# The last sums of regrouped rows on VectorE, and two regrouping transfers asked for by GpSimd, at the end of a global-filter and SoLU kernel

## The chip, the cores and the metric

The kernel runs on one core of one Trainium2 chip. Its time is the device time of one execution in microseconds, and a kernel is judged by the median of its runs. The kernel before the change was run three times: 1555.18, 1557.51 and 1562.97 us, so its median is 1557.51 us. One more execution was profiled; every row of the profile below is from that one.

Five engines work beside each other: PE (TensorE, the matmuls, with PEld for its weight loads), DVE (VectorE), ACT (ScalarE), POOL (GpSimd) and SP (SyncE, which here only issues DMA transfers). Each takes its instructions in the order in which the program puts them. DMA transfers are issued by SP, ACT or POOL, and all of them run on the same 16 DMA engines.

## The reference, cut to what matters

```
# x: 8 x 3136 x 256; filters: 1569 x 256; 25088 tokens of 256 afterwards
X = rfft(x, axis=1);  y = irfft(X * (filt_r + 1j * filt_i), n=3136, axis=1)
t = y.reshape(25088, 256)
h = t @ w_in                                  # 25088 x 1024
sm = exp(h - max(h)) / (sum(exp(h - max(h))) + 1e-9)
solu = h * sm
ln = (solu - mean(solu)) / sqrt(var(solu) + 1e-6) * g_ln
out = ln @ w_out                              # 25088 x 256
```

## The kernel before, in words

**Blocks, pairs, groups.** The tokens are cut into 196 blocks of 128. Two blocks are a pair (98 pairs, numbered 0 to 97) and four are a group. For a pair, both matrix products are done by Strassen's scheme in Winograd's form: seven products of half-size blocks in place of eight, at the price of sums of blocks ahead of them. `product` does the first matrix product (128x512 tiles), `project` the second.

**One step.** `step(k)` runs for k = 0 to 204 and writes down, engine by engine, everything of one step; the order of its lines is the order on every engine. A step does the first product of block k, exponential, normalization and square of blocks k-2 and k-3, and one half of the second product of an older pair. Spectrum work of later batches is spread over the steps. Block 195, the last, has its first product in step 195. Steps 196 to 204 have no new block: there the pairs 93 to 97 are brought to their end. They are called the tail here.

**From rows to the second product.** The 1024 values of a token lie along a row, and the second product needs them as columns. `turn(k)` (L945) transposes 32x32 pieces on DVE into the group's tile `turn`. When all four blocks of a group are turned, `regroup(p, i)` (L953) collects block i of pair p into a tile `solu_t`: four DMA transfers of 128 KB, one for each quarter of the destination's partitions. The pairs 96 and 97 belong to the same group, so all their 16 transfers become possible at the same moment, when block 195 is turned. In this document 96/0 and 96/1 are the two tiles of pair 96, and 96/1 q2 is the third quarter of the second.

**Sums and products of a pair.** `project_sums` (L991) makes four tiles of 128x512 out of the two: s1 = a21 + a22 and s2 = s1 - a11 in its step 0, a21 = a11 - a21 (called s3, in place) and s4 = a12 - s2 in its step 1. Here a11 and a12 are the halves of tile 0, a21 and a22 those of tile 1: s1 needs tile 1 alone, the other three need both. All go through `sum_of` (L853), which puts them on POOL. The second product of a pair is written 95:4 for product 4 of pair 95; each product is 8 matmuls of 128x128. An odd step has p:1 (a11), p:2 (a12), p:6 (s2) and p:7 (s3), the even step after it p:5 (s1), p:3 (s4) and p:4 (a22). Products 1, 6 and 5 add into one PSUM bank, 2, 7 and 4 into another, and product 3 of the last five pairs has one of its own.

**Between the products.** After some products the bank is read before the next product adds to it: `keep_out` (L1036, ACT) and `finish_out` (L1040, DVE) scale a bank by the rows' deviation and add. Thus p:4 waits for the `finish_out` that reads the second bank after p:7, and (p+1):2 waits for the `finish_out` that reads it after p:4. `regroup_deviations` (L984) uses PE for a small matmul between two pairs, whose result ACT copies; (p+1):1 comes after that copy. `store_out` (L1045) writes a pair's result to memory with two transfers by SP.

**The tail's order.** Step 198 has, among others, on POOL: s1 and s2 of pair 95, then s3 and s4 of pair 95, then the transfers 97/1 q2 and q3, then the three small operations of `deviations` (L975). On DVE: one `finish_out` of pair 94, `turn(195)`, and the two remaining `finish_out` of pair 94. On ACT: the transfers 96/1 q0 and q1. On SP: 96/0 q0 to q3, 96/1 q2 and q3, 97/0 q0 to q3, 97/1 q0 and q1, then the stores. Step 199 has 95:1, 95:2, 95:6 and 95:7. Step 200 begins with s1 and s2 of pair 96; then come 95:5, the `finish_out` ahead of 95:4, 95:3, 95:4, the small matmul, s3 and s4 of pair 96, and the last two `finish_out` of pair 95. Step 201 has 96:1, 96:2, 96:6 and 96:7, and step 202 does for the pairs 96 and 97 what step 200 did for 95 and 96. Steps 203 and 204 are the products of pair 97.

**Waits of transfers.** A transfer counts on a semaphore when it has landed. SP and ACT share eight such semaphores, taken in turn, so that an issue can also wait until the transfer that had the same semaphore before has landed.

Of the kernel before, what the change touches and what calls it, by code (L numbers as in the profile page):

```python
# [13 lines left out]
ALU = mybir.AluOpType  # L14
# [96 lines left out]
def kernel(  # L111
# [10 lines left out]
    nc = tc.nc  # L122
# [727 lines left out]
    def tokens(k, c):  # L850
        return y[:, c, P * (k % NT):P * (k % NT) + P]

    def sum_of(out, in0, in1, op):  # L853
        nc.gpsimd.tensor_tensor(out=out, in0=in0, in1=in1, op=op)  # L854

    def pair_sums(j):

# [95 lines left out]
    def regroup(p, i, dma=nc.sync.dma_start, parts=range(4)):  # L953


        g, second = divmod(p, 2)
        turned = turns[g].rearrange("p (k q) b i -> p k q (b i)", q=4)
        a = 2 * second + i
        if (p, i) not in regrouped:
            if p == last[-1]:  # L960
                st = pools["r"].tile([P, KF, P], FP32, name=f"solu_t_{p}_{i}", tag="r")
            else:
                st = upool.tile([P, KF, P], FP32, name=f"solu_t_{p}_{i}", tag=f"solu_t{i}")
            regrouped[p, i] = st
            solu_ts[p, i] = st[:, 0:KF // 2, :], st[:, KF // 2:KF, :]
        for q in parts:
            dma(out=regrouped[p, i][32 * q:32 * q + 32, :, :], in_=turned[32 * a:32 * a + 32, :, q, :])  # L967
# [23 lines left out]
    def project_sums(p, step):  # L991

        (a11, a12), (a21, a22) = solu_ts[p, 0], solu_ts[p, 1]
        if step == 0:
            s1 = upool.tile([P, KF // 2, P], FP32, name=f"u1_{p}", tag="u1")
            s2 = spool.tile([P, KF // 2, P], FP32, name=f"u2_{p}", tag="u2")
            sum_of(s1, a21, a22, ALU.add)
            sum_of(s2, s1, a11, ALU.subtract)
            solu_sums[p] = s1, s2
        else:  # L1000
            s4 = spool.tile([P, KF // 2, P], FP32, name=f"u4_{p}", tag="u4")
            s1, s2 = solu_sums[p]
            sum_of(a21, a11, a21, ALU.subtract)
            sum_of(s4, a12, s2, ALU.subtract)
            solu_sums[p] = s1, s2, a21, s4

    def project(p, m):
# [136 lines left out]
    pairs = blocks // 2  # L1144

    def step(k):
        j, odd = divmod(k, 2)
        p = j - (LAG - 1) // 2 if odd else j - (LAG + 1) // 2
        if not 0 <= p < pairs:
            p = None  # L1150
        hid, proj = k < blocks, p is not None
        sums_of_x = differences[k] + products[k]
        if not odd and k > LAG:
            for job in sums_of_x:
                job()
            sums_of_x = []
        if not odd and 2 <= j - 4 < pairs:
            project_sums(j - 4, 0)
        plain = j < DIRECT
        if plain:  # L1160
            direct(2 * j, odd)
            if k == 0:
                convert_w_out(0)
        elif k < LAG:
            if not odd:
                product(j, 1)
                keep(j, k, 0)
                product(j, 2)
                finish(j, k, 0, (k, 0), 1)
            else:  # L1170
                product(j, 5)
                keep(j, k - 1, 1)
                finish(j, k, 1, (k - 1, 1), 2)
        for job in top[k] + (sums_of_x + stores[k] if k < LAG else stores[k] + sums_of_x):
            job()
        if not odd and 0 <= j - 4 < 2:
            project_sums(j - 4, 0)
        if odd and DIRECT <= j + 1 < pairs:
            pair_sums(j + 1)
        if not odd:  # L1180
            if hid and k > LAG:
                product(j, 1)
                keep(j, k, 0)
            if 2 <= k < blocks:
                exponential(k - 2)
            if proj:
                project(p, 5)
                keep_out(p, 1, (1, 1) if p in last else (0, 1))
            if p in last:
                keep_out(p, 0, (0, 1))  # L1190
                finish_out(p, 1, 1, (1, 1), 1)
            if blocks <= k < blocks + 2:
                exponential(k - 2)
            if hid and k > LAG:
                product(j, 2)
            if 3 <= k < blocks + 3:
                turn(k - 3)
            if hid and k > LAG:
                finish(j, k, 0, (k, 0), 1)
            if proj and p not in last:  # L1200
                finish_out(p, 1, 1, (0, 1), 1)
            for job in early[k]:
                job()
            if k == 6:
                w_out_mean()
            if 3 <= k < blocks + 3:
                square(k - 3)
            if plain:
                direct(2 * j + 1, 0)
            elif hid:  # L1210
                product(j, 6)
                keep(j, k + 1, 0)
            if proj:
                project(p, 3)
                if p not in last:
                    keep_out(p, 0, (0, 1))
                project(p, 4)
            if j >= 4 and j % 2 == 0 and j - 4 < pairs:
                regroup_deviations((j - 4) // 2, places.pop(p) if proj else psum("ps_rs")[:, 0, 0:4])
            for job in spectrum_loads[k]:  # L1220
                job()
            if 0 <= j - 3 < pairs - 2:
                regroup(j - 3, 0)
                regroup(j - 3, 1)
            elif j - 3 == pairs - 2:
                regroup(j - 3, 1, nc.scalar.dma_start, range(2))
                regroup(j - 3, 0)
                regroup(j - 3, 1, parts=range(2, 4))
                regroup(j - 2, 0)
                regroup(j - 2, 1, parts=range(2))  # L1230
            if 0 <= j - 4 < pairs:
                project_sums(j - 4, 1)
            if j - 3 == pairs - 2:
                regroup(j - 2, 1, nc.gpsimd.dma_start, range(2, 4))
            if 0 <= j - 3 < pairs and j % 2:
                deviations((j - 3) // 2)
            if hid and not plain:
                product(j, 7)
            if p in last:
                finish_out(p, 0, 1, (0, 1), 2)  # L1240
                finish_out(p, 1, 0, (1, 0), 1)
                store_out(p)
            if 2 <= k < blocks + 2:
                normalize(k - 2)
            for job in second_parts[k] + middle[k] + first_parts[k]:
                job()
            if proj and p not in last:
                finish_out(p, 1, 0, (1, 0), 1)
                store_out(p)
        else:  # L1250
            if hid and k >= LAG:
                product(j, 5)
                keep(j, k - 1, 1)
                finish(j, k, 1, (k - 1, 1), 2)
            for job in early[k]:
                job()
            if proj:
                project(p, 1)
                keep_out(p, 0, (0, 0))
                project(p, 2)  # L1260
                finish_out(p, 0, 0, (0, 0), 1)
            if 2 <= k < blocks + 2:
                exponential(k - 2)
            if plain:
                direct(k, 1)
            elif hid:
                product(j, 3)
                product(j, 4)
            if proj:
                project(p, 6)  # L1270
                project(p, 7)
            for job in second_parts[k] + middle[k]:
                job()
            if 3 <= k < blocks + 3:
                turn(k - 3)
            if hid and not plain:
                finish(j, k - 1, 1, None, 0)
                finish(j, k, 0, (k, 0), 2)
            if 2 <= k < blocks + 2:
                normalize(k - 2)  # L1280
            if proj:
                keep_out(p, 1, (1, 0))
            if 3 <= k < blocks + 3:
                square(k - 3)
            for job in first_parts[k]:
                job()
        if k == 6:
            center_w_out()
        if 7 <= k < LAG:
            for n in range(2 * k - 14, 2 * k - 12):  # L1290
                weight_sum(nc.vector, w_out_sb, n)
        for job in late[k] + loads[k]:
            job()
        if k == 5:
            weight_sum(nc.vector, w_in_sb, 3)
            w_out_sums()
        if k < 3:
            convert_w_out(k + 1)
        for n in {1: (0,), 2: (1,), 3: (2,), 4: (3,)}.get(k, ()):
            scale_w_out(n)  # L1300
        if k == 4:
            nc.gpsimd.dma_start(out=turn_t, in_=turn_dram)
# [35 lines left out]
```

## Time and profile before

| | |
|---|---|
| three runs | 1555.18, 1557.51, 1562.97 us |
| profiled execution, its own time | 1558.44 us |
| its span, first to last instruction | 1556.7 us |
| mean granted TensorE clock | 0.997 |
| PE busy | 1534.5 us (99%) |
| DVE, POOL, ACT busy | 1241.3, 1107.3, 923.3 us |
| tail: block 195 turned on DVE | 1526.61 us |
| tail: last matmul ends | 1551.45 us |
| POOL tensor_tensor, 128x512, alone | 1.26 us |
| DVE tensor_tensor, 128x512, both inputs in SBUF (L172), alone | 0.68 us |

Times in the tables and rows count from the start of the span. A row of the timeline has its start, its length, the engine, the source line, the operation with out<-in by the program's tile names (`u` for the sums, `solu_t` for regrouped tiles, `turn` for turned blocks, `ot` and `o` for the results), the count of instructions merged in it, and in brackets the idle time of the engine before it with what ended that. SPq and ACTq are the engines' sequencers, which issue transfers. A row of the stretches has, behind the stretch, its length and the busy time of PE, PEld, DVE, ACT and POOL with the count of instructions, then the granted TensorE clock (1.00 is full speed), the mean busy share of the 16 DMA engines and the GB/s that they moved.

### The profile page before, as it was taken

Reading aid. Unit: us, or ns where it says so; the run is one execution under the profiler, and the core shown is the slowest. Engines: PE = TensorE matmul, PEld = TensorE weight load, DVE = VectorE, ACT = ScalarE, POOL = GpSimd, SP = SyncE. Lnnn points to the kernel's source line nnn. Section 1 sums busy time; section 2 is a strip of 40 time slices with the busy share of each in tenths; the row PEclk is TensorE's granted clock in tenths of the full one; section 3 lists DMA queues with packets and bytes.
Section 4 is the critical chain, followed back from the end, with each engine's and each line's share of the span. In section 5 each row is a group of like instructions: output and inputs, shape, how many; then the busy total and the mean of one; then the engine's idle time right before and its main releaser. Section 6 shows DMA issues by size and latency. Waiting matters only on the chain. (4 is left out here: it accounts for less than half of the span.)

```text
span 1556.7 us, 36704 instructions
## 1 busy us (share of the span) xinstructions
PE 1534.5 (99%) x12922; PEld 1066.0 (68%) x12922; DVE 1241.3 (80%) x2220; ACT 923.3 (59%) x1893; POOL 1107.3 (71%) x1290
## 2 busy tenths in 40 slices
PE   9999999999999999999999999999999999999997
PEld 6735676666666776667666776667676777777777
DVE  5888878988988798868897699877987777777772
ACT  4556565665556565665656555665656656666662
POOL 2226776797879776986689678996767766676665
PEclk9999999999999999999999999999999999999999
DMA  9779587867986788667886678766874544344444
GB/s 250 267 254 274 160 229 218 238 196 212 245 242 188 188 247 238 198 164 202 248 230 183 166 209 246 209 181 185 228 206 118 135 122 121 97 119 105 107 109 109
DMA packets 340831, 297.58 MB, mean 191 GB/s; under 512 B 27313, under 2 KB 310731, under 8 KB 340649
## 3 DMA queue, kind: packets, MB, share of 16 engines
q1 hardware_dynamic: 277864, 175.33, 42.4%
q0 software_dynamic: 29152, 87.33, 18.7%
q10 hardware_dynamic: 33634, 32.58, 7.1%
q8 instruction: 105, 1.72, 0.5%
q14 instruction: 76, 0.62, 0.1%
HBM read 117.53 MB, written 74.84 MB: 124 GB/s over the span
## 5 line engine op out<-in xcount | busy, mean ns | idle before, releaser
L1022 PEld LDWEIGHTS o<-w_out_sb,solu_t 128*128 128x128 f32 x3136 | 381.7, 192 | 49.9 <-issue 43.1
L1022 PE MATMUL o<-w_out_sb,solu_t 128*128 128x128 f32 x3136 | 401.3, 276 | 3.7 <-DVE ot L1042 3.1
L1022 PEld LDWEIGHTS o<-w_out_sb,u 128*128 128x128 f32 x2352 | 307.3, 192 | 138.3 <-issue 108.6
L875 PE MATMUL m<-w_in_sb,s 128*128 128x512 f32 x760 | 384.5, 607 | 2.4 <-ACT h L896 1.6
L1022 PE MATMUL o<-w_out_sb,u 128*128 128x128 f32 x2352 | 310.7, 276 | 2.3 <-POOL u L854 1.8
L932 DVE SCALAR_TENSOR_TENSOR h<-e,h 128x1024 f32<-128x1024 f32 x196 | 304.5, 1554 | 0.0
L875 PE MATMUL m<-w_in_sb,y 128*128 128x512 f32 x570 | 297.1, 603 | 1.7 <-DVE h L907 1.2
L1038 ACT ACTIVATE ot<-o,rs_t 128x128 f32<-128x128 f32 x392 | 143.2, 367 | 244.6 <-PE o L1022 242.8
L896 ACT COPY h<-m 128x512 f32<-128x512 f32 x285 | 167.7, 588 | 200.5 <-PE m L875 179.7
L854 POOL TENSOR_TENSOR u<-solu_t 128x512 f32<-128x512 f32 x98 | 135.2, 1380 | 186.7 <-DMA solu_t<-turn 131.0
L910 DVE CUSTOM_DVE_ANT_0 h<-m,h 128x512 f32<-128x512 f32 x190 | 130.1, 685 | 166.8 <-ACT h L896 104.0
L940 ACT ACTIVATE h<-h,nmu 128x1024 f32<-128x1024 f32 x196 | 224.9, 1147 | 41.8 <-DVE turn L950 41.7
L950 DVE STREAM_TRANSPOSE turn<-h 128x1024 f32<-128x1024 f32 x196 | 243.2, 1241 | 3.2
L920 ACT ACTIVATE e<-h,nmax 128x1024 f32<-128x1024 f32 x196 | 225.3, 1149 | 9.3 <-DVE h L932 7.9
L854 POOL TENSOR_TENSOR u<-solu_t,u 128x512 f32<-128x512 f32 x98 | 136.9, 1396 | 99.6 <-PE o L1022 99.3
L1042 DVE SCALAR_TENSOR_TENSOR ot<-o,rs_t,ot 128x128 f32<-128x128 f32 x299 | 103.8, 347 | 100.1 <-ACT ot L1038 61.4
L875 PEld LDWEIGHTS m<-w_in_sb,s 128*128 128x128 f32 x760 | 124.5, 191 | 80.3 <-issue 63.0
L854 POOL TENSOR_TENSOR u<-u,solu_t 128x512 f32<-128x512 f32 x98 | 162.6, 1659 | 16.8 <-PE o L1022 7.6
L854 POOL TENSOR_TENSOR solu_t<-solu_t,solu_t 128x512 f32<-128x512 f32 x98 | 155.6, 1587 | 0.9
L875 PEld LDWEIGHTS m<-w_in_sb,y 128*128 128x128 f32 x570 | 93.6, 190 | 89.6 <-issue 45.9
L854 POOL TENSOR_TENSOR s<-y 128x128 f32<-128x128 f32 x190 | 94.4, 497 | 0.5
L437 PEld LDWEIGHTS py<-wb_t,t 50*64 50x64 f32 x3584 | 57.6, 134 | 42.9 <-issue 19.4
(153 smaller groups left out, 1939.0 us busy)
## 6 DMA issues: line engine op xcount, KB each, us to landing
solu_t<-turn SPq DMA_DIRECT2D x780, 128.0 KB
out_dram<-ot SPq DMA_DIRECT2D x196, 128.0 KB
t<-d POOLq DMA_DIRECT2D x112, 200.0 KB, 6.7
t<-d ACTq DMA_DIRECT2D x37, 512.0 KB
f<-f_dram POOLq DMA_DIRECT2D x37, 512.0 KB, 7.9
d<-g POOLq DMA_DIRECT2D x36, 512.0 KB, 4.8
d<-x POOLq DMA_DIRECT2D x80, 200.0 KB, 5.2
de<-de_tbl ACTq DMA_DIRECT2D x37, 256.0 KB
```

The costliest lines, as they stand in the source:

```text
L437: nc.tensor.matmul(out=views[g][64 * h:64 * h + 64, cb, i, :], lhsT=t4[rows, i, c0:c0 + 64], rhs=wb_t[rows, 0:N1], start=True, stop=True)
L854: nc.gpsimd.tensor_tensor(out=out, in0=in0, in1=in1, op=op)
L875: nc.tensor.matmul(out=ms[j, bank], lhsT=lhsT, rhs=w_in_sb[:, w, :], start=m in (1, 2, 7), stop=True, skip_group_check=True)
L896: nc.scalar.copy(out=h_half(k, i), in_=ms[j, 0])
L910: nc.vector.tensor_tensor_reduce(out=h_half(k, i), in0=ms[j, bank], in1=h_half(*kept), scale=1.0, scalar=sofar, op0=ALU.add, op1=ALU.min, ...
L920: nc.scalar.activation(out=e, in_=hs[k], func=AFT.Exp, bias=nmaxs.pop(k)[:, 1:2], scale=-1.0, accum_out=esums[g][:, i:i + 1])
L932: nc.vector.scalar_tensor_tensor(out=solu, in0=e, scalar=SHRINK, in1=solu, op0=ALU.mult, op1=ALU.mult, accum_out=nmu)
L940: nc.scalar.activation(out=solu, in_=solu, func=AFT.Square, bias=nmu, scale=-float(DFF), accum_out=variances[g][:, i:i + 1])
L950: nc.vector.transpose(out=turns[g][:, :, i, :], in_=solus[k].rearrange("p (f j) -> p f j", j=32))
L1022: nc.tensor.matmul(out=pos[p, bank], lhsT=lhs[:, f, :], rhs=w[:, f, :], start=f == 0 and (m in (1, 2, 7) or alone), stop=True, skip_group_ ...
L1038: nc.scalar.activation(out=out_half(p, *to)[0], in_=pos[p, 0], func=AFT.Copy, scale=rs)
L1042: nc.vector.scalar_tensor_tensor(out=ot, in0=pos[p, bank], scalar=rs, in1=out_half(p, *kept)[0], op0=ALU.mult, op1=ALU.add)
```

## The change

Three things change, all in the tail.

- `project_sums` gets an engine: VectorE where p + step is 96 or more. These are all four sums of the pairs 96 and 97, and s3 and s4 of pair 95. Each stays at the same place of the program's order, now in DVE's queue.
- The transfers 96/1 q2 and q3 are issued by POOL in place of SP. They stand in step 198 right behind the two that ACT issues, and so in POOL's queue behind s1 and s2 of pair 95.
- On SP, 97/0 follows directly on 96/0.

```diff
-    def sum_of(out, in0, in1, op):
-        nc.gpsimd.tensor_tensor(out=out, in0=in0, in1=in1, op=op)
+    def sum_of(out, in0, in1, op, engine=nc.gpsimd):
+        engine.tensor_tensor(out=out, in0=in0, in1=in1, op=op)
...
         (a11, a12), (a21, a22) = solu_ts[p, 0], solu_ts[p, 1]
+        engine = nc.vector if p + step >= pairs - 2 else nc.gpsimd
         if step == 0:
...
-            sum_of(s1, a21, a22, ALU.add)
-            sum_of(s2, s1, a11, ALU.subtract)
+            sum_of(s1, a21, a22, ALU.add, engine)
+            sum_of(s2, s1, a11, ALU.subtract, engine)
...
-            sum_of(a21, a11, a21, ALU.subtract)
-            sum_of(s4, a12, s2, ALU.subtract)
+            sum_of(a21, a11, a21, ALU.subtract, engine)
+            sum_of(s4, a12, s2, ALU.subtract, engine)
...
                 regroup(j - 3, 1, nc.scalar.dma_start, range(2))
+                regroup(j - 3, 1, nc.gpsimd.dma_start, range(2, 4))
                 regroup(j - 3, 0)
-                regroup(j - 3, 1, parts=range(2, 4))
                 regroup(j - 2, 0)
```

## The prediction

> **What bounds the kernel now.** First the page, for the engine that is always busy: it is PE, so only time in which PE idles or runs slowly can change.
>
> ```profile
> span 1556.7 us, 36704 instructions
> ...
> PE 1534.5 (99%) x12922; PEld 1066.0 (68%) x12922; DVE 1241.3 (80%) x2220; ACT 923.3 (59%) x1893; POOL 1107.3 (71%) x1290
> ```
>
> The change touches nothing ahead of step 198. Second, then, the chain that ended last, from 1520 us on: block 195 is turned at 1526.61, an ACT transfer and then an SP transfer land (1535.37), POOL makes s1, s2 and s3 of pair 96, and from 1539.41 on PE runs without a wait.
>
> ```profile
> 1527.70 3.52 DMA solu_t<-turn
> ...
> 1531.24 4.13 DMA solu_t<-turn
> ...
> 1536.87 1.26 POOL u L854
> 1538.13 1.23 POOL solu_t L854
> ...
> 1539.41 12.05 PE o L1022 x88
> ```
>
> Third, the timeline of the tail, for what each engine waits for: PE idles 0.56 us ahead of 95:6 (1529.01), 0.35 ahead of 96:1 (1534.40), 1.76 ahead of 96:6 (1538.18, for s2 of pair 96).
>
> ```profile
> 1525.51 2.94 PE L1022 MATMUL o<-w_out_sb,solu_t 128*128 128x128 f32 x24 [0.18 <-DVE ot L1042]
> 1526.53 0.57 DVE L1042 SCALAR_TENSOR_TENSOR ot<-o,rs_t,ot 128x128 f32<-128x128 f32 x2
> ...
> 1529.33 1.30 POOL L967 DMA_DIRECT2D solu_t<-turn  x2
> ...
> 1532.37 0.35 DVE L1042 SCALAR_TENSOR_TENSOR ot<-o,rs_t,ot 128x128 f32<-128x128 f32 x1 [3.12 <-ACT ot L1038]
> ...
> 1532.77 1.16 PE L1022 MATMUL o<-w_out_sb,solu_t 128*128 128x128 f32 x8
> ...
> 1534.40 2.02 PE L1022 MATMUL o<-w_out_sb,solu_t 128*128 128x128 f32 x16 [0.35 <-DMA solu_t<-turn]
> 1535.53 1.26 POOL L854 TENSOR_TENSOR u<-solu_t 128x512 f32<-128x512 f32 x1 [3.07 <-DMA solu_t<-turn]
> ...
> 1538.18 1.16 PE L1022 MATMUL o<-w_out_sb,u 128*128 128x128 f32 x8 [1.76 <-POOL u L854]
> ```
>
> Fourth, stretches of 3.41 us, for the clock: right after the stretch with that idle time, PE's granted clock is 0.50 for 3.41 us. The grid of stretches is set by the two times at which the clock changed. Three busy for 1.46 to 1.59 us of 3.41 (two of them shown) were followed by half clock; one busy for 1.86 was not. So a stretch in which PE idles for more than about 1.7 us costs half of the next 3.41 us, 1.7 us.
>
> ```profile
> 1536.27:1539.68 3.41, 1.59 (x12) 1.24 (x11) 0.35 (x1) 0.30 (x1) 3.33 (x4) 1.00 0.50 131
> 1539.68:1543.09 3.41, 3.41 (x18) 3.41 (x18) 0.00 (x0) 0.14 (x2) 3.33 (x3) 0.50 0.27 91
> ...
> 89.03:92.44 3.41, 1.46 (x4) 0.74 (x5) 3.38 (x7) 0.01 (x1) 0.00 (x0) 1.00 0.53 205
> 92.44:95.85 3.41, 3.41 (x6) 1.26 (x5) 3.17 (x8) 0.73 (x2) 0.00 (x0) 0.50 0.77 244
> 430.36:433.77 3.41, 1.86 (x5) 0.93 (x6) 2.66 (x6) 1.98 (x4) 2.04 (x3) 1.00 1.03 343
> 433.77:437.18 3.41, 3.41 (x41) 2.59 (x39) 3.38 (x6) 1.53 (x4) 1.38 (x3) 1.00 1.05 245
> ```
>
> **The change part by part.** *The length of a sum.* Ten sums of 1.26 us leave POOL. The same shape with both inputs in SBUF took DVE 0.68 us alone (L172); beside POOL's work the L172 rows reach a median of 1.16 and a maximum of 1.76. From 1531 us on POOL has nothing left to do, so I take 0.68, and 0.6 from start to start (DVE's rows overlap by 0.08).
>
> *s3 and s4 of pair 95.* They stand in DVE's queue between turn(195) and the last two finish_out of pair 94, the second of which frees the bank for 95:2. DVE is free at 1526.61, but POOL's s2 of pair 95 runs to 1526.94, and where a normalization on DVE started beside a sum on POOL (1503.06, 2.27 us against 1.22 alone) it ended one operation's length after POOL did. So s3 ends at 1527.6, s4 at 1528.2, the finish_out at 1528.5 and 1528.8 (before: 1527.1). 95:1 ends at 1527.35; 95:2 starts at 1528.8, an idle time of 1.45 us, and with it goes the 0.56 ahead of 95:6. PE is then 0.7 us behind, and 95:3 ends at 1533.3 (before: 1532.6). Bounds: 0 if DVE gets in beside POOL's last 0.3 us, 2.0 if POOL's transfer issues also hold it. None reaches the end, by the next step.
>
> *s1 and s2 of pair 96.* They now stand in DVE's queue ahead of the finish_out that 95:4 waits for (before: 1532.37, and 95:4 right behind it). s2 needs all of 96/0. Call the landing of its last transfer L; before, PE's 96:1 was released by it at 1534.3. s1 needs only 96/1 and runs earlier. So s2 ends at L + 0.7, the finish_out at L + 1.05, and there 95:4 starts: PE idles from 1533.3. From 95:4 to 96:1 it was 1.63 us (1532.77 to 1534.40: the small matmul and ACT's copy lie between), and that stays. Behind 96:1 come 14 products; at full clock one follows another by 0.895 us (1546.60 to 1548.39 for two), and the last takes 1.16, so the last matmul ends 1.63 + 13 x 0.895 + 1.16 = 14.4 us after 95:4's start, at L + 15.5. The waits of before inside this stretch go: s2, s3 and s4 of pair 96 are made beside 95:4 and 96:1. finish_out of pair 95, behind s3 and s4, ends at about L + 2.9, and 96:2 wants its bank at L + 3.6; pair 97's has less, some 0.1 us.
>
> *The transfers.* 96/1 q2 and q3 go out on POOL at 1527.0 instead of on SP at 1530.53 and 1531.24, and 97/1 q2 and q3 follow at 1528.3 and 1529.0 (0.65 each, from the 1.30 for two), instead of 1529.33 and 1530.03. By POOL's 3.8 to 4.2 us to landing 96/1 is complete at about 1532, not 1535.37. SP has ten issues instead of twelve, its stores of pair 94 come some 1.3 us sooner, and nobody waits for them. deviations on POOL moves up by 1 us, without effect.
>
> What it does to L is not in the trace. The 16 transfers moved 2.1 MB at 211 GB/s from 1528 to 1538 us, DMA share 0.73 to 1.13: the engines are the limit, and the change only reorders. Before, what had landed by L = 1534.3 were eight transfers, with two nearly done. Now 96/0 shares with the two of ACT and all four of POOL: ten. And SP's fourth issue waits for ACT's first transfer to land:
>
> ```profile
> SPq L967 <- DMA solu_t<-turn: 1.1, 1, 1.1
> ```
>
> Ten transfers of 131 KB at 211 GB/s from 1528.0 are 6.2 us, L = 1534.2; a wait for a slower landing of ACT's transfer pushes it. Lower end: the fourth issue at 1529.85 as before and 2.4 us to landing, as the first took on free engines, L = 1532.3. Upper end: ACT's first lands 2 us later (1531.9) and the fourth takes its 4.4 us of before, L = 1536.3. I take 1534.7, nearest to the row of before, with a little for four transfers on POOL ahead of it.
>
> *Clock.* With L = 1534.7 PE idles from 1533.3 to 1535.75 and again for 0.6 us ahead of 96:1. A grid of 3.41 us that lies anywhere has a stretch with over 1.7 us of that idle time in six cases of seven. So half clock once again, as in the profiled execution.
>
> *The sum*, against that execution: the last matmul ends at 1534.7 + 15.5 + 1.7 = 1551.9, where it ended at 1551.45. Behind it come the same finish_out, store and ends. 1558.44 + 0.45 = 1558.9 us. The profiled execution stands 0.9 us above the median of the runs, 1557.51; since it had the half clock and other runs may not have had it, I make no correction, and the forecast is 1.4 us above the median: no change that can be measured.
>
> **The rivals.** *The clock stays full.* The Trainium skill (TensorE: Matmul & The Clock Gate, the table on why this matters for your kernels) asks for idle gaps of over about 3 us before the clock falls; 1.8 us in 3.41 sufficed here, so the trace goes against it. As a mechanism of this kernel: the gap of 2.45 us is split by the grid, or too short, and nothing is lost. Then 1558.9 - 1.7 = 1557.2 us. For it: one case of seven by the grid, more if L is early; against it: the rows above.
>
> *The gain that DVE's shorter sums offer.* 96/0 lands by about 1532.3 to 1533, so DVE is through s2 before 95:3 ends, 95:4 waits little, and no stretch idles for 1.7 us. The last matmul ends at 1547.8 to 1548.5, 3.0 to 3.6 us sooner: 1554.8 to 1555.5 us. If DVE could run the finish_out ahead of s2, PE would be bound by the landing alone (96:1 at 1534.4, end 1547.2): 1554.2. For it: four transfers are asked for earlier, and SP's queue is shorter. Against it: the DMA engines are already full.
>
> *Slower: the wait on DVE is longer than the one on POOL that it replaces.* It decides from L = 1534.3 on with half clock, from 1535.9 without. POOL's transfers push those of SP: from 1531 to 1532 us, POOL's queue moved 0.12 MB with 32 packets and SP's 0.08 MB with 171. With L = 1536.3 it is 1560.5 us; if 96/0 came last of all 16, L = 1538.3, 1562.5. Against it: POOL's are 0.5 MB and pass in 2.5 us. The Trainium skill (DMA: Bandwidth & Descriptors, queues, rings and completion order) says that an engine takes whole packets from the queues in turn; those packets of some 4 KB against 512 B agree, and by that rule alone SP would have about a tenth of the engines until 1531.5, L about 1535.5 and 1559.7 us.
>
> **How the numbers follow.** Chances: the forecast 0.45 (L from 1533.8 to 1535.6 at half clock: 1558.0 to 1559.8), full clock 0.2, the gain 0.15, slower 0.2. The range takes in the middle of the gain and most of the slower case, and runs differ by some us among themselves (three span 7.8): 1553.8 to 1562.2. Less than 0.5% (7.8 us), about what a measurement of this kernel can tell from no change, is all that any case gives; the three idle times above and the slow clock together are 4.4 us. I leave 0.03 for faster and 0.04 for slower by more, for a spread of the runs like the one shown.
>
> **What would show it.** In the profile after: DVE rows of 0.68 us for the sums; PE idle ahead of 95:2 for about 1.4 us on a finish_out; PE idle ahead of 95:4 for about 2.4 us, ended by a finish_out that ran right behind s2; no idle time ahead of 96:6; 96/1 landed before 96/0; half clock for 3.41 us somewhere from 1536 on. It is wrong if 96/0 lands more than 1 us from 1534.7, if DVE's order differs from the program's, or if PE idles inside 96 and 97.

## The result, and the profile after

| | before | after |
|---|---|---|
| median of 22 runs each | 1559.62 us | 1563.45 us |
| ratio, 95% interval | | 1.0023 [1.0012, 1.0034] |
| profiled execution, its own time | 1558.44 us | 1565.15 us |
| its span | 1556.7 us | 1563.4 us |

The change made the kernel slower by 0.23%: 3.6 us by the ratio, 3.83 by the medians. That is under the 0.5% within which the prediction put any change, but it is a loss clear of the noise where no measurable change was forecast, and 1563.45 us lies above the range.

Block 195 was turned at 1526.60 us before and at 1529.40 us after. Those 2.8 us lie ahead of everything that the change touches; kernels that are alike up to there had it anywhere between 1525.28 and 1533.73 us in the executions profiled below. So all times of the tail below count from the end of that turn. "The tail" is from there to the end of the last matmul: 24.84 us before, 28.36 us after, 3.52 us more. So the two profiled executions show the size of loss that the medians show.

The page of after, its first lines: PE is still the engine that is always busy, DVE has the ten sums more; POOL has ten sums less and two transfer issues more.

```profile
span 1563.4 us, 36701 instructions
...
PE 1537.0 (98%) x12922; PEld 1069.0 (68%) x12922; DVE 1241.0 (79%) x2230; ACT 923.9 (59%) x1893; POOL 1097.2 (70%) x1282
```

The timeline of after's tail, with what each engine waited for:

```profile
1530.06 2.45 POOL L967 DMA_DIRECT2D solu_t<-turn  x4 [0.32 <-issue]
1530.21 0.68 DVE L854 TENSOR_TENSOR u<-solu_t,u 128x512 f32<-128x512 f32 x1
...
1531.46 1.16 PE L1023 MATMUL o<-w_out_sb,solu_t 128*128 128x128 f32 x8 [1.11 <-DVE ot L1043]
...
1535.54 0.69 DVE L854 TENSOR_TENSOR u<-solu_t 128x512 f32<-128x512 f32 x1 [2.47 <-DMA solu_t<-turn]
1539.83 0.69 DVE L854 TENSOR_TENSOR u<-u,solu_t 128x512 f32<-128x512 f32 x1 [3.60 <-DMA solu_t<-turn]
1540.44 0.35 DVE L1043 SCALAR_TENSOR_TENSOR ot<-o,rs_t,ot 128x128 f32<-128x128 f32 x1
...
1540.84 2.07 PE L1023 MATMUL o<-w_out_sb,solu_t 128*128 128x128 f32 x8 [4.64 <-DVE ot L1043]
```

PE waits twice: 1.11 us ahead of 95:2 (1531.46) and 4.64 us ahead of 95:4 (1540.84). Both waits name a `finish_out`. The second one stood on DVE behind s2 of pair 96 (1539.83), and s2 stood waiting 3.60 us for a transfer. The three waits of before (0.56, 0.35 and 1.76) are gone, ahead of 96:6 too. The chain that ended last says which transfer:

```profile
1532.79 6.92 DMA solu_t<-turn
...
1539.83 0.69 DVE u L854
1540.52 0.27 DVE ot L1043
...
1540.84 2.07 PE o L1023 x8
...
1543.13 14.64 PE o L1023 x112
```

It is 96/0 q3, SP's fourth, issued at 3.38 and landed 6.92 us later, at 10.31. Before, it was issued at 3.25 and landed at 7.66. Last the clock, in stretches on its own grid of 3.41 us (length, PE's busy time and matmuls, granted clock, DMA share, GB/s):

```profile
1532.68:1536.09 3.41, 3.41 (x32) 1.00 0.89 207
1536.09:1539.51 3.42, 0.10 (x1) 1.00 1.08 235
1539.51:1542.92 3.41, 2.08 (x10) 0.50 0.49 126
1542.92:1546.33 3.41, 3.41 (x16) 0.50 0.26 84
1546.33:1549.75 3.42, 3.42 (x32) 1.00 0.05 17
```

The long wait brought not one stretch at half clock, as before, but two.

### The profile page after: what moved, and what is told of

Its sections match the earlier page's. It is cut to its first block, busy times and chain, and to the rows that moved or that the text cites. A ratio compares the mean times of both kernels' runs of the same rounds, so it can differ in the third digit from the quotient of the medians.

```text
span 1563.4 us, 36701 instructions
## 1 busy us (share of the span) xinstructions
PE 1537.0 (98%) x12922; PEld 1069.0 (68%) x12922; DVE 1241.0 (79%) x2230; ACT 923.9 (59%) x1893; POOL 1097.2 (70%) x1282
## 5 line engine op out<-in xcount | busy, mean ns | idle before, releaser
L854 POOL TENSOR_TENSOR solu_t<-solu_t,solu_t 128x512 f32<-128x512 f32 x95 | 149.6, 1575 | 0.9
```

Of the source, the lines that this page charges most:

```text
L854: engine.tensor_tensor(out=out, in0=in0, in1=in1, op=op)
```

## The experiments

Two theories stood against each other. **A:** the loss is the place of s1 and s2 on DVE: the `finish_out` that frees 95:4's bank waits behind sums that wait for transfers, and POOL's transfers make the last one of 96/0 late. **B:** it is DVE's own work, or the transfers alone. (The expectations on record letter their theories anew for each run.) For each run: when 96/0 and 96/1 were complete, PE's idle time (waits over 0.08 us, summed), half clock inside the tail, the tail, the rest of it (PE's own time), and the kernel's median against that of the kernel before on the same chip.

| run | 96/0 | 96/1 | idle | half clock | tail | PE's own | median | ratio |
|---|---|---|---|---|---|---|---|---|
| before | 7.66 | 8.76 | 2.67 | 3.41 | 24.84 | 22.17 | | |
| before_again | 7.94 | 8.72 | 2.64 | 0 | 23.30 | 20.66 | -0.85 | 0.9991 [0.9976, 1.0005] |
| after | 10.31 | 6.12 | 5.75 | 6.83 | 28.36 | 22.61 | +3.83 | 1.0023 [1.0012, 1.0034] |
| after_again | 9.10 | 6.11 | 4.55 | 6.83 | 27.37 | 22.82 | +3.10 | 1.0017 [1.0002, 1.0032] |
| e1_sums_only | 6.74 | 8.22 | 4.44 | 6.83 | 27.41 | 22.97 | +3.17 | 1.0019 [0.9998, 1.0040] |
| e6_behind_sp | 6.63 | 8.16 | 1.55 | 0 | 22.56 | 21.01 | -1.81 | 0.9988 [0.9975, 1.0001] |
| e2_transfers_only | 7.55 | 6.72 | 0.84 | 0 | 21.75 | 20.91 | -3.39 | 0.9984 [0.9970, 0.9997] |
| e2b_transfers_only | 8.66 | 6.59 | 1.53 | 0 | 21.98 | 20.45 | -0.60 | 0.9991 [0.9975, 1.0006] |
| e3_sums_behind | 8.81 | 6.09 | 2.29 | 0 | 22.93 | 20.64 | +2.11 | 1.0017 [1.0000, 1.0035] |
| e3b_sums_behind | 8.87 | 6.11 | 2.36 | 3.41 | 24.63 | 22.27 | +2.01 | 1.0010 [0.9995, 1.0025] |
| e4_two_on_pool | 7.49 | 6.02 | 2.93 | 3.41 | 24.56 | 21.63 | +0.88 | 1.0000 [0.9984, 1.0016] |
| e7_fetch_early2 | 8.72 | 6.62 | 4.17 | 3.41 | 25.78 | 21.61 | +1.56 | 0.9997 [0.9982, 1.0012] |
| e8_fill | 8.74 | 6.59 | 1.11 | 0 | 24.50 | 23.39 | +0.56 | 1.0006 [0.9992, 1.0021] |
| e5_fetch_early | 9.33 | 6.67 | 4.77 | 6.83 | 27.49 | 22.72 | +13.87 | 1.0100 [1.0074, 1.0126] |

The last column but two sorts itself: 20.5 to 21.0 us without half clock in the tail, 21.6 to 22.3 with one stretch, 22.6 to 23.0 with two (e8 has 24 matmuls more). So a stretch of half clock costs 0.6 to 1.8 us, and two cost 1.6 to 2.5.

### One part of the change alone

**e1_sums_only**: the sums on DVE, the transfers by the same engines and in the same order as before. With s3 and s4 of pair 95 gone from POOL, its transfers 97/1 q2 and q3 still go out sooner, at 0.30 and 1.00 us where it was 2.73 and 3.43.

```diff
                 regroup(j - 3, 1, nc.scalar.dma_start, range(2))
-                regroup(j - 3, 1, nc.gpsimd.dma_start, range(2, 4))
                 regroup(j - 3, 0)
+                regroup(j - 3, 1, parts=range(2, 4))
```

> Only the sums go to VectorE; all transfers are issued as before the change. Lengths are counted from the end of the turn of block 195: the last matmul ended at 24.84 us before the change and at 28.36 after it; the last transfer of 96/0 landed (L) at 7.66 before and 10.30 after. Theory A (the order on VectorE makes PE wait for L, and the transfers on GpSimd make L late): L is as before, about 7.7; PE waits ahead of 95:4 until L + 1.1; the last matmul ends at L + 15.5 at full clock, 23.2, or 24.9 to 26.6 with one or two stretches of half clock. Theory B (the order on VectorE alone is the loss): about 28.4 whatever the transfers do. Theory C (the transfers alone are the loss): PE does not wait ahead of 95:4, 21 to 23 us.

**e2_transfers_only**: the two transfers of 96/1 by GpSimd, all sums on POOL, as before. The diff is against the kernel before.

```diff
                 regroup(j - 3, 1, nc.scalar.dma_start, range(2))
+                regroup(j - 3, 1, nc.gpsimd.dma_start, range(2, 4))
                 regroup(j - 3, 0)
-                regroup(j - 3, 1, parts=range(2, 4))
```

> Only 96/1 q2 and q3 go to GpSimd; all sums stay there, so that s3 and s4 of pair 95 run behind these two transfers and 97/1 q2, q3 behind the sums. Counted from the end of the turn of block 195. Theory A: no finish_out waits behind a sum, so 95:4 is not held; 96/1 lands at about 4 to 6 us, 97/1 is asked for 2.5 us later than in the changed kernel and passes behind 96/0, so L is 7.7 to 9; 96:1 starts at L and the last matmul ends at L + 12.9, 20.6 to 22 at full clock against 24.84 before: a gain of 2 to 4 us. Theory C (the transfers alone are the loss): L is about 10.3 as in the changed kernel, PE idles ahead of 96:1 by 2.6 us and the clock falls, 25 us or more.

**e1**: tail 27.41 us, above the 23.2 to 26.6 that theory A gave: I had left out that s1, at the head of DVE's queue, needs 96/1, which SP now brings last. The timeline:

```profile
1536.26 0.69 DVE L854 TENSOR_TENSOR u<-solu_t 128x512 f32<-128x512 f32 x1 [4.68 <-DMA solu_t<-turn]
1537.04 0.69 DVE L854 TENSOR_TENSOR u<-u,solu_t 128x512 f32<-128x512 f32 x1
...
1538.05 2.08 PE L1023 MATMUL o<-w_out_sb,solu_t 128*128 128x128 f32 x8 [3.34 <-DVE ot L1043]
```

96/0 was there at 6.74 us, earlier than before the change, and yet PE waited 3.34 us ahead of 95:4. The sums alone cost what the whole change costs (+3.17 us against +3.83 and +3.10, though the interval of e1 just reaches no change). So a late 96/0 is not needed for the loss: here it was 96/1 that held s1, and s1 that held the `finish_out`.

**e2**: tail 21.75 us, the shortest of all, and faster than before by 0.16% [0.03%, 0.30%]. 96/1 is complete at 6.72 instead of 8.76, so POOL has s2 of pair 96 sooner and the wait ahead of 96:6 falls from 1.76 to 0.29 us:

```profile
1538.84 1.26 POOL L854 TENSOR_TENSOR u<-u,solu_t 128x512 f32<-128x512 f32 x1
...
1540.15 1.16 PE L1022 MATMUL o<-w_out_sb,u 128*128 128x128 f32 x8 [0.29 <-POOL u L854]
```

So the transfers alone, which theory B also had under suspicion, cost nothing.

The same kernel again:

> The transfers-only kernel once more (two regroupings of 96/1 asked for by GpSimd, all sums left on GpSimd), with more rounds. If its gain is real: ratio to the kernel before 0.997 to 0.9997, in the profile 96/0 landed at 7.2 to 8 after the end of the turn of block 195, idle ahead of 96:6 under 0.7 us and no half clock in the tail, tail 21.5 to 23. If the first measurement was chance: ratio above 0.9997 with the same tail, or a tail of 24 and more.

Tail 21.98 us as expected, ratio 0.9991 [0.9975, 1.0006]: the same sign, without being told from no change by itself. The kernel before, measured against itself, gave 0.9991 too. So the gain in the tail is shown twice (1.3 to 3.1 us under the two tails of before), that in the whole time once.

### The sums' place in DVE's queue

**e6_behind_sp**: e1, with the sums behind the `finish_out` instructions of the pair before. **e3_sums_behind**: the same move in the changed kernel; **e3b** is e3 again.

```diff
-        if not odd and 2 <= j - 4 < pairs:
+        if not odd and 2 <= j - 4 < pairs - 2:
             project_sums(j - 4, 0)
...
-            if 0 <= j - 4 < pairs:
+            if 0 <= j - 4 < pairs - 3:
                 project_sums(j - 4, 1)
...
                 finish_out(p, 1, 0, (1, 0), 1)
                 store_out(p)
+                if pairs - 2 <= j - 4 < pairs:
+                    project_sums(j - 4, 0)
+                if pairs - 3 <= j - 4 < pairs:
+                    project_sums(j - 4, 1)
```

> The regroupings as before the change (two of 96/1 asked for by SyncE), and the ten sums on VectorE, but behind the finish_outs of the pair before in VectorE's queue. Counted from the end of the turn of block 195. Theory A (what the change loses is the finish_outs' place behind sums that wait for a transfer): no idle time of PE ahead of 95:2 and 95:4 over 0.4 us, 96/0 landed at 6.5 to 7.6, 96/1 at 8.2 to 8.8, s2 of pair 96 ready by 10.2, idle ahead of 96:6 under 0.6 instead of 1.76, no half clock in the tail; the last matmul ends at 21 to 22.5 against 24.84 before the change, and the time is 2 to 4 us under that of the kernel before. Theory B (VectorE's work itself, or its instruction fetch, slows the transfers or the finish_outs): 96/0 lands at 8.5 or later, or idle times of over 1 us inside pairs 95 and 96; the time is no better than before.

> The changed kernel, with the sums on VectorE put behind the finish_out of the pair before (s3 and s4 of pair 95, and all of pairs 96 and 97); the transfers are those of the change. Counted from the end of the turn of block 195. Theory A: PE waits neither ahead of 95:2 nor ahead of 95:4; it waits ahead of 96:1 for L, which stays at about 10.3, by some 2.6 us; the last matmul ends at L + 12.9 + up to 0.5 = 23.2 to 23.7 at full clock and 25 to 27 with half clock, against 28.36. Theory C (order on VectorE does not matter): 28.4 as in the changed kernel.

> The kernel with the sums on VectorE behind the finish_outs and the transfers of the change, once more, because its profile (tail 22.93) and its median (above that of the kernel before) disagreed. Theory A (the tail is what differs, and the first median was drift ahead of the tail): tail 22 to 24.5, ratio 0.9975 to 1.0. Theory B (its other executions have a half clock in the tail that the profiled one had not): tail 25 to 27 with one or two stretches of half clock, ratio 1.0 to 1.003.

e1 and e6 differ only in this move; their transfers landed alike (6.74 and 8.22, 6.63 and 8.16). The timeline of e6:

```profile
1539.95 1.16 PE L1023 MATMUL o<-w_out_sb,solu_t 128*128 128x128 f32 x8
...
1542.00 0.69 DVE L854 TENSOR_TENSOR u<-solu_t 128x512 f32<-128x512 f32 x1 [0.19 <-DMA solu_t<-turn]
1542.73 0.69 DVE L854 TENSOR_TENSOR u<-u,solu_t 128x512 f32<-128x512 f32 x1
...
1543.57 1.13 PE L1023 MATMUL o<-w_out_sb,u 128*128 128x128 f32 x8 [0.44 <-DVE u L854]
```

95:4 (1539.95) starts without a wait, the sums run after it, and what is left is 0.62 and 0.44 us. The tail is 22.56 against 27.41 us, the median 1.81 us under before against 3.17 above. The same ten sums on the same engine: the loss is their place in the queue, not their work, and theory B is out for DVE. (Each median is against the kernel before on its own chip, and both intervals just reach no change; the tails are one execution each.)

e3 removes the wait ahead of 95:4 in the same way. It keeps one of 1.5 us ahead of 96:1, for 96/0, which lands 2.2 us later than in e6 with four of POOL's transfers ahead of it. Its tail was 22.93 and 24.63 us, about what before's two were; its medians were 2.1 and 2.0 us above before. The two don't contradict each other: both profiled executions (1556.22 and 1559.58 us) lie far below e3's medians (1563.06 and 1562.52) and are not typical. Every run lists the granted clock of its whole execution. Both profiled ones had 0.999, but 14 of the 22 runs of e3 and e3b had 0.997 or less. The runs with 0.998 or more, three and five of them, have medians of 1558.96 (e3) and 1560.60 us (e3b), those of the kernel before on the same chips 1559.63 and 1560.28. So what e3 loses goes with the half clock, as theory B of e3b's expectation had it. In e3b's profile one stretch of it stands right behind the wait ahead of 96:1; of an execution at 0.997 or less there is no profile.

### How many transfers go ahead of 96/0

**e4_two_on_pool**: the changed kernel, with 97/1 q2 and q3 left to SP, at the end of its list.

```diff
-                regroup(j - 2, 1, parts=range(2))
+                regroup(j - 2, 1)
...
-            if j - 3 == pairs - 2:
-                regroup(j - 2, 1, nc.gpsimd.dma_start, range(2, 4))
```

> The changed kernel, but the last two transfers of tile 97/1 are asked for by SyncE, at the end of its list, and not by GpSimd; GpSimd asks for two of the sixteen instead of four. Counted from the end of the turn of block 195. Theory A (the transfers on GpSimd's queue pass ahead of the last one of 96/0, so their number sets its landing): two transfers of 131 KB less pass ahead of it, at 211 GB/s 1.2 us, so 96/0 lands at 8.6 to 9.3 instead of 10.31; product 95:4 starts 1.1 later than the later of 96/0 and 96/1; the last matmul ends at 25.5 to 27.2 with one or two stretches of half clock; the time is 1 to 3 us under that of the changed kernel. Theory B (the instruction fetch on one DMA engine alone made the landing late): 96/0 still lands at 10.0 or later and the tail stays at 28 or above. Theory C (the queue that is left longer on SyncE holds something else, 97/1, that is needed in time): a new idle time of PE ahead of a product of pair 97, tail above 28.4.

The chain of waits of e4, then of the changed kernel's second execution, each with its row for 96/0 q3:

```profile
1535.79 4.10 DMA solu_t<-turn
...
1540.02 0.69 DVE u L854
```

```profile
1533.15 5.73 DMA solu_t<-turn
```

With two transfers less on POOL's queue, 96/0 landed at 7.49, against 8.72 to 9.10 in the executions of the same order with four in which no 16-KB fetch of instructions (the next section) began between the turn and the landing (after_again, e3, e3b, e7, e8). (96/0 was expected at 8.6 to 9.3, because that was reckoned from the 10.31 of the first profile; the next section shows what made it so late.) Two transfers at 211 GB/s are 1.24 us, and the difference is 1.2 to 1.6. e2, in which POOL's sums hold back its last two transfers to 4.41 and 4.99 us, has 7.55. So theory A's second half holds: what POOL asks for early makes SP's fourth late. Counting bytes is not the whole of it: in e1 and e6 POOL also asks for two early, and 96/0 landed at 6.74 and 6.63, 0.8 us sooner than in e4. Why is open. Tail 24.56 us, even a little shorter than expected, and a median of 0.88 us above before.

### The late last share of 96/0

In the first profile of after, 15 of the 16 shares of 96/0 q3 had landed at 9.13 and the last at 10.31. The list of DMA queues for 1535.7 to 1536.9 us has one packet of 16 KB with instructions in it:

```profile
q0 software_dynamic: 84, 0.24, 74.2%
q1 hardware_dynamic: 147, 0.07, 26.0%
q8 instruction: 1, 0.02, 5.2%
```

5.2% of 16 engines' 1.2 us is 1.0 us of one engine. The last share of this transfer and of SP's next four landed 0.7 to 1.2 us behind the 15th. The row does not say for which engine the instructions were. I took it for DVE's own instructions, which the change has more of, and tried to move it with 30 one-column memsets on VectorE, one in each of the steps 100 to 129.

> The changed kernel with 30 more VectorE instructions of 1 element per partition, one in each of the steps 100 to 129. In the changed kernel 15 of the 16 engines' shares of 96/0 q3 had landed at 8.7 to 9.1 us after the turn of block 195 and the last at 10.30; a 16 KB transfer of instructions of 0.99 us ran in between (1535.8 us), when VectorE was at the instruction at which it ran at 1548.2 before the change. Theory D (that fetch is VectorE's, it comes every 256 of its instructions, and it holds one DMA engine): with 30 more instructions it falls ahead of the transfers, L is 8.8 to 9.1 and the last matmul ends 1.2 to 1.5 us sooner than 28.36, or 3 us sooner if one stretch of half clock goes with it. Theory E (the late share has nothing to do with fetches): L stays at about 10.3. The 30 instructions themselves cost nothing that can be seen, VectorE being busy for 79%.

> The changed kernel and 30 one-column memsets on VectorE, one in each of steps 100 to 129, into a column of a small constant that nothing reads; no new tile, so that every address in SBUF stays as it was. VectorE's instruction fetch comes some 30 instructions sooner, ahead of the last regroupings. Counted from the end of the turn of block 195. Theory A (the fetch delays the last share of 96/0, and the 13 us of the run with a new tile came from the shifted addresses): 96/0 lands at 8.8 to 9.5 with its shares together, 95:4 starts 1.1 later, tail 26.5 to 27.7, and the time is 0.5 to 2 us under that of the changed kernel. Theory B (the memsets themselves cost the 13 us): the time is 10 us or more above that of the changed kernel, with the drift beginning at step 100. Theory C (the fetch does not matter): 96/0 lands at 10.0 or later although the fetch is earlier.

**e5** wrote into a new tile, **e7** into a column that nothing reads of a constant that is there already:

```diff
 # e5
+    pad = small.tile([P, 1], FP32, name="pad", tag="pad")
...
+        if 100 <= k < 100 + 30:
+            nc.vector.memset(pad, 0.0)
 # e7
+        if 100 <= k < 100 + 30:
+            nc.vector.memset(small_consts[:, 7:8], 0.0)
```

Both had the 16-KB fetch elsewhere and 96/0 complete at 9.33 and 8.72. But that says nothing of the memsets, as the next run showed, the changed kernel itself once more:

> The changed kernel once more, for the spread of its tail. Counted from the end of the turn of block 195. Theory A (the late last shares of 96/0 came from an instruction fetch that fell between the transfers by chance): the fetch comes elsewhere, 96/0 lands at 8.6 to 9.3, 95:4 starts 1.1 later, the tail is 25.5 to 27.7 instead of 28.36, and the ratio to the kernel before stays at 1.000 to 1.003. Theory B (the fetch belongs to the change): it comes at 6.4 again, 96/0 lands at 10 or later, tail 28 to 28.7.

Its fetch came at -2.17 us, ahead of the transfers, with no memset at all, and 96/0 landed at 9.10. The two executions of e2 show the same from the other side: one kernel, its fetch at -2.16 in one and at 6.08 us in the other, and 96/0 at 7.55 and 8.66. So the fetch costs the transfer that it falls on 1.1 to 1.2 us. Where it falls differs between executions of one kernel, so it is no part of the change, and nothing shows that it was DVE's. Without it the changed kernel's tail was still 27.37 us.

e7's whole time was 1.56 us above before, where after and after_again were 3.83 and 3.10 above; that the memsets cost nothing is all that it shows. e5's was 13.87 above, and the turn of block 195 came 13.1 us later than in before. With e7 beside it, that goes with the new tile, not with the memsets' number. From 200 to 600 us, e5 and then e7:

```profile
200.00:600.00 400.00, 392.89 (x3780) 1.00 0.84 219
```

```profile
200.00:600.00 400.00, 396.15 (x3881) 1.00 0.80 222
```

The DMA engines were busier (0.84 against 0.80) for no more bytes per second (219 and 222 GB/s), and PE less. I suppose that the tile moved other tiles' places in memory; that wasn't tested.

### The clock

**e8_fill**: the changed kernel, with product 95:3 computed four times instead of once, so that PE has 2.7 us of work more just where it would wait.

```diff
                 project(p, 3)
+                if p == pairs - 3:
+                    for _ in range(3):
+                        project(p, 3)
```

> The changed kernel, in which product 95:3 is computed four times over into its own bank (the same values), so that TensorE works 2.7 us longer in the time in which it would wait ahead of 95:4. Counted from the end of the turn of block 195. Theory A (idle time in a stretch of 3.41 us brings the half clock): the gap ahead of 95:4 falls from 3.1 to 4.6 to 0.3 to 1.9, no half clock in the tail, or one stretch of 3.41 if 96/0 lands at 10 or later; tail 24.0 to 26.7, 1.7 to 3.4 us less than that of the changed kernel, although TensorE does 24 more matmuls. Theory B (the half clock is set by something other than TensorE's idle time, such as the transfers): the half clock stays, tail as in the changed kernel or above.

The stretches of e8:

```profile
1529.97:1533.38 3.41, 3.35 (x30) 1.00 0.91 217
1533.38:1536.79 3.41, 3.30 (x27) 1.00 1.12 235
1536.79:1540.21 3.42, 3.42 (x33) 1.00 0.35 94
```

Full clock throughout, no wait ahead of 95:4, and a tail of 24.50 against 27.37 us although PE does 24 matmuls more. The median was 2.54 us under that of the changed kernel on the same chip (1561.07 and 1563.61). The transfers were as dense as ever (DMA share 1.12), so it is PE's idle time that brings the half clock. The other runs bear it out: the granted clock of the whole execution was 0.997 or less in 8 of the 12 runs of after_again, and in none of e8's 12. One stretch of 3.41 us at half clock lowers it by 0.0011 (half of 3.41 out of 1557). The 2.9 us are 2.1 from PE's own time (22.82 against 23.39 less the 2.69 us of the added products), and 0.75 because the waits shrank by 3.44 us, more than the 2.69 put in.

When does one stretch become two? The stretches of after_again, of e7 and of e3b:

```profile
1535.72:1539.13 3.41, 0.84 (x8) 1.00 1.11 250
1539.13:1542.54 3.41, 2.53 (x12) 0.50 0.72 154
1542.54:1545.96 3.42, 3.42 (x18) 0.50 0.27 93
1545.96:1549.37 3.41, 3.41 (x32) 1.00 0.08 27
```

```profile
1535.10:1538.51 3.41, 0.37 (x4) 1.00 1.08 244
1538.51:1541.92 3.41, 3.39 (x16) 0.50 0.51 130
1541.92:1545.34 3.42, 3.42 (x32) 1.00 0.26 85
```

```profile
1533.44:1536.86 3.42, 1.86 (x16) 1.00 1.08 246
1536.86:1540.27 3.41, 3.41 (x18) 0.50 0.73 156
1540.27:1543.68 3.41, 3.41 (x32) 1.00 0.27 91
```

A half-clock stretch in which PE was busy almost throughout (3.39, 3.41) was followed by full clock; one with idle time at its head (busy 2.53 here, 2.08 in after, 2.83 in e1) by another at half clock. In e7 the wait happened to end on the grid, and its tail is 1.6 us shorter than that of after_again, with 96/0 only 0.38 us earlier.

### The kernel before, again

> The kernel before once more, for the spread of its tail and as a measure of what two medians of the same kernel differ by. Theory A (the profiled execution is typical): 96/0 landed at 7.3 to 7.9 after the end of the turn of block 195, gaps 0.56, 0.35 and 1.76, half clock for 3.41 us, tail 24.8. Theory B (it was an unlucky one): no half clock in the tail, tail 23.0 to 23.3. The ratio within 0.9985 to 1.0015 either way.

Tail 23.30 us, without half clock: its longest wait was 1.45 instead of 1.76 us, and the stretch with it was busy for 2.02 us.

```profile
1533.26:1536.68 3.42, 2.02 (x16) 1.00 0.84 198
1536.68:1540.09 3.41, 3.19 (x26) 1.00 0.26 80
```

So the profiled execution of before, against which the prediction was summed, had half clock in its tail; this one did not, and is 1.5 us shorter there. The profiled execution of before had a granted clock of 0.997; of the 93 other runs of before that list it, 26 had that or less. Of the 34 runs of the changed kernel, 25 had.

## Why the prediction was wrong

**The length of a sum: right.** 0.68 to 0.69 us on DVE, 0.6 from start to start; only s3 of pair 95, beside POOL's last sum, took 0.96.

**s3 and s4 of pair 95: right.** The wait ahead of 95:2 was 1.11 us (forecast 1.45, between 0 and 2.0), and the later waits hid it, as said.

**From the landing to the end: right.** 95:4 started 1.13 us after 96/0 had landed in after and after_again and in e7 (forecast 1.05). The last matmul was put at the landing plus 15.5 plus 1.7 for one stretch of half clock. With e7's landing that gives 25.9 us (measured 25.78) and with e4's 24.7 (24.56). Nothing waited inside the pairs 96 and 97.

**What the change does to the landing: the first step that failed.** The prediction took 1534.7, which is 8.1 us after the turn, as the value nearest to the row of before. Undisturbed, 96/0 landed at 8.7 to 9.1: the two transfers of 97/1 that POOL asks for early cost 1.2 to 1.6 us (e4), and the 4.4 us of SP's fourth became 5.3 to 5.7. "A little for four transfers on POOL" was too little by 0.6 to 1.0 us. In the profiled execution the fetch added 1.2 more, which nothing in the trace of before announced. The estimate by the rule that engines take packets from the queues in turn (the Trainium skill, DMA: Bandwidth & Descriptors, queues, rings and completion order) was 1535.5, or 8.9 us. The undisturbed runs agree with it better than with mine, which fits the rule but does not show it. The suspected wait of SP's fourth issue was hardly a part of it: it was issued at 3.38 us, against 3.25 before.

**The clock: the second step that failed.** Half clock came again, as forecast and against the rival with full clock. It came twice over, which no case of the prediction had. The term of 1.7 us, half of one stretch, was for one stretch only: 27.5 us by its own formula with the landing at 10.31, and 28.36 measured; 26.3 and 27.37 in after_again. That is 0.9 to 1.1 us. The Trainium skill (TensorE: Matmul & The Clock Gate, Part 1, the table of the two states) has the full clock return after a busy window of about 3.4 us; the stretches above agree. Read as a window that has to be busy throughout, that would have given the second stretch for a wait that runs into the slow one. The same table has the clock fall after an idle window of about 3.4 us; that doesn't hold here, where in e3b a stretch with 1.56 us of wait in it sufficed. Nor does the prediction's limit of 1.7 us hold exactly: a stretch busy for 1.86 us was followed by full clock in its rows and by half clock in e3b, and one busy for only 1.47 by full clock (e4, from 452.92 us).

**The sum.** Against a tail of 25.3 us that the forecast meant (24.84 + 0.45), after had 28.36: 2.2 from the landing and 0.9 from the clock. after_again had 27.37: 1.0 and 1.1. The medians differ by 3.83 us where 0.45 was forecast. What is left of the miss of 4.55 us is the base: the three runs shown had a median of 1557.51 us, the profiled one 1558.44, and 22 runs 1559.62. And the half clock that the prediction set against a half clock of before is in only one of the two profiles of before. From the tail of before_again to that of after_again it is 4.07 us: the 0.45 of the forecast, 1.0 from the landing, 1.1 from the second stretch of half clock, and 1.5 for a first one that this execution of before had not. That is near the 3.1 to 3.8 us of the medians.

**The rivals.** What happened is the case that was called slower, at 0.2, by the mechanism that it names, a wait on DVE longer than the one on POOL that it replaces. Its break-even, the landing at 1534.3 (7.7 us) with half clock, was passed by 1.0 to 2.6 us. The gain's condition, 96/0 landed by 5.7 to 6.4 us after the turn, was met in no run (6.63 at the earliest); it failed on that and on the `finish_out` behind s2, not on the sums' length. e6, in which DVE runs the `finish_out` ahead of s2, and e2, which leaves the sums on POOL, come near the times of that case: tails 2.3 and 3.1 us under that of before's profile, where it had 3.0 to 4.2. Of that, 1.5 us is half clock that before_again hadn't either.

## What to carry to other kernels

Before an operation that waits for a transfer is moved to a faster engine, look at what stands behind it in that engine's queue: here 0.57 us saved per sum cost a wait of 3 to 5 us, because a 0.35-us instruction that PE needed stood behind the sums, and behind that instruction the same sums cost nothing. Transfers that are asked for early on one queue can make those on another late: here two of them 1.2 to 1.6 us, where their bytes over the measured rate are 1.24. And price an idle time of PE with the clock that follows it: 0.6 to 1.8 us for a stretch here, and a second one where the wait reaches into the slow stretch.

## What the runs showed of the hardware

- A fetch of 16 KB of instructions holds one of the 16 DMA engines for 0.9 to 1.4 us. When it falls among transfers that are spread over all 16, those on their way then are complete later, the one that matters here by 1.1 to 1.2 us (e2 and e2b: 96/0 at 7.55 and 8.66). Where it falls differs between executions of one kernel.
- Half clock lasts until a stretch of 3.41 us has been busy almost throughout: in the fourteen profiles, half-clock stretches inside the kernel busy for 2.08 to 2.83 us were each followed by another, those busy for 3.31 (e1, from 452.03 us) and more by full clock.
- In the same profiles, every full-clock stretch in which PE was busy for less than 1.47 us was followed by half clock, and every one busy for more than 1.86 by full clock. In between both occur: 1.77 (e6, from 456.42 us) and 1.86 (e3b) went to half clock, 1.47 (e4, from 452.92) and 1.60 (e2, from 89.10) stayed at full. What decides there is open. In the tail of before, the stretch with the longest wait was busy for 1.59 us in one execution, which had half clock and took 24.84 us, and for 2.02 in the other, which had none and took 23.30.
- A new tile of one column changed the DMA share from 0.80 to 0.84 at about the same GB/s and the kernel's time by some 13 us. How is open.
